# Order of the first loads in a state-space and gated-FFN kernel: activations and first weight groups dealt anew to two DMA queues

## The chip, the cores and the metric

The kernel runs on one core of a Trainium2 chip. A core has TensorE (PE, matrix products, with its weight loads PEld), VectorE (DVE), ScalarE (ACT), GpSimd (POOL), and SyncE (SP), which only issues DMA transfers here. ACT and POOL issue transfers too; each of the three has a DMA queue of its own, and the transfers of all are carried out by the core's 16 DMA engines. The metric is the device time of one execution in microseconds, as the median of several runs. The profile is of one execution, taken by the hardware profiler.

## The reference

The input x has 2048 rows of 512 elements in bfloat16. It is normalised row by row, and the sum of x and two branches is returned:

```python
xn = _layernorm(x, axis=-1)
return x + _A_ref(xn, ...) + _B_ref(xn, w_gate, w_up, w_down)

# A: a diagonal state-space layer, P = 512 complex states
Bu = jnp.einsum("bld,pd->blp", x + 0j, B_bar)
h = Lam_bar[None, :] * h + Bu[:, t, :]        # for each of the 2048 rows
y = 2.0 * jnp.einsum("blp,dp->bld", hseq, Cmat).real + x * Dskip[None, None, :]

# B: a gated feed-forward layer, F = 1376
g = _silu(x @ w_gate)
u = x @ w_up
return (g * u) @ w_down
```

## The kernel before

The 2048 rows are 16 tiles of 128 rows (`xall[:, n, :]`, tile n), and four chunks of four tiles. A chunk goes through these stages: layer norm on VectorE (`ln_stats`, `ln_rstd`, `norm_dve`, lines 174 to 189), transposition to `xnT`, the gate and up products by groups of 128 columns (`gu_mm`, line 408), the projections of the state-space layer (`bproj_tile`, line 333), rotations and scans on VectorE, and the output products (lines 488 and 497). The order on each engine is written out by hand: instructions stand on an engine in the order in which the program calls them, and a semaphore makes one wait for its inputs.

Gate and up weights are loaded in groups of columns: `fgroups = [(0, 2), (2, 4), (4, 7), (7, FT - 1)]`. Group 0 holds the column tiles 0 and 1, group 1 the tiles 2 and 3. A group of gate weights is called wg0, wg1 and so on here, a group of up weights wu0, wu1. Tiles x0 to x3 are the first chunk; a tile has 128 KB, each of the groups 0 and 1 has 256 KB, in rows of 512 bytes; rows of x have 1024 bytes. `load_w1(q, tiles, view, gi)` issues the load of group gi on the queue q; its instruction has line 112 for all groups.

The first loads are issued by SP and ACT, one behind the other on each. x0 is split over the two by partitions. Then SP issues x1, wg0, x2, wg1, x4 to x7 in one transfer, and the later groups; ACT issues wu0, x3 and wu1, and is then free for its own work. From SP's fifth load on, each issue on SP waits until the load that was issued eight loads earlier, over both queues, has landed.

The head of the program, written out at its end, is made so that TensorE can begin with single tiles of 128 rows before the chunk is complete. Eleven matmuls of 512 columns on a zeroed tile (`dummy(11, CW)`) come first. Then, in this order:

```python
    ln_stats(0)
    ln_rstd(0, 1)
    ln_stats(1)
    norm_dve(0)
    ln_rstd(1, 2)
    xT_pe(0)
    dummy(11, 128)
    ln_stats(2)
    norm_dve(1)
    ln_rstd(2, 3)
    head_mm(0, 0)
    xT_pe(1)
    head_mm(1, 0)
    head_mm(2, 0)
    ln_stats(3)
```

`ln_stats(n)` (lines 175 and 176) reads tile n and so waits for its load. `ln_rstd` is an addition on VectorE (line 179) and a power on POOL (line 180). `norm_dve(n)` (line 188) writes the normalised tile back to `xall`. On VectorE the statistics of tile n + 1 stand ahead of the normalisation of tile n. `xT_pe(n)` (line 200) transposes tile n by four matmuls into PSUM, and ACT (line 204), or VectorE for tile 3 (line 202), copies the result to `xnT`. `head_mm(fi, i)` computes column tile fi of gate and up for the 128 rows of tile i: eight matmuls of 128 columns. `head_mm(0, i)` and `head_mm(1, i)` use group 0, `head_mm(2, i)` uses group 1. The head goes on with tiles 2 and 3 in the same manner; from column tile 3 on whole chunks of 512 columns are worked on.

Of the kernel before, what the change touches and what calls it, by code (L numbers as in the profile page):

```python
# [23 lines left out]
def kernel(  # L24
# [17 lines left out]
    nc = tc.nc  # L42
# [36 lines left out]
    x_v = A_x[0].rearrange("(n p) d -> p n d", p=128)  # L79
    out_v = out[0].rearrange("(n p) d -> p n d", p=128)  # L80
    wg_v = B_w_gate.rearrange("(k p) f -> p k f", p=128)
# [3 lines left out]
    xall = const.tile([128, NT, D], BF16, name="xall")  # L85
# [3 lines left out]
    wg_g, wu_g = [], []  # L89
# [20 lines left out]
    def load_w1(q, tiles, view, gi):  # L110
        a, b = fgroups[gi]
        q.dma_start(out=tiles[gi][:], in_=view[:, :, a * 128:min(F, b * 128)])  # L112
# [1 line left out]

    nc.sync.dma_start(out=xall[0:64, 0, :], in_=x_v[0:64, 0, :])  # L115
    nc.scalar.dma_start(out=xall[64:128, 0, :], in_=x_v[64:128, 0, :])
    nc.sync.dma_start(out=xall[:, 1, :], in_=x_v[:, 1, :])  # L117
    load_w1(nc.scalar, wu_g, wu_v, 0)
    load_w1(nc.sync, wg_g, wg_v, 0)
    nc.scalar.dma_start(out=xall[:, 3, :], in_=x_v[:, 3, :])  # L120
    nc.sync.dma_start(out=xall[:, 2, :], in_=x_v[:, 2, :])
    load_w1(nc.scalar, wu_g, wu_v, 1)
    load_w1(nc.sync, wg_g, wg_v, 1)
    prm_rows = const.tile([3 * NQ, 128], BF16, name="prm_rows")
# [620 lines left out]
```

## Time and profile before

| | |
|---|---|
| median of 3 runs | 183.5 us (182.9 to 183.63) |
| profiled execution | 183.73 us, its span 181.7 us |
| PE busy | 175.3 us (96%) |
| DVE busy | 152.9 us (84%) |
| ACT busy | 93.4 us (51%) |
| POOL busy | 25.6 us (14%) |
| chain that ended last | PE 93%, DMA 3%, SPq 1%, DVE 1% |
| of it the load of x | 3.0% |
| DMA | 15.53 MB, 85 GB/s on average |

Times in the profile are microseconds from the start of the span. The chain that ended last is followed back from the last instruction, at each step to what released it. A group's idle time is that of its engine just before it, with the cause. "SPq" and "ACTq" are the issuing queues of SP and ACT; for a DMA issue, the time to landing runs from the start of the issue to the moment when the data are there. The matmuls' busy time is modelled, and pipelined matmuls overlap.

### The profile page before, as it was taken

The numbers are of one execution on the slowest core, as the hardware profiler recorded it, in microseconds if no ns is written. First come the engines' busy times: TensorE is split into PE (matmuls) and PEld (weight loads), VectorE is DVE, ScalarE is ACT, GpSimd is POOL, SyncE is SP. The second block draws the span as 40 slices with busy tenths as digits, with TensorE's granted clock in tenths as the row PEclk, the third lists the DMA queues.
The fourth block names the chain that finished last, engine by engine and source line by source line (L and its number), as shares of the span: only waits on it lengthen the run. The fifth ranks groups of instructions, "written<-read, shape, count | busy, mean of one in ns | idle before, by whom it ended". The sixth has DMA issues, their size and how long they took to land.

```text
span 181.7 us, 2449 instructions
## 1 busy us (share of the span) xinstructions
PE 175.3 (96%) x914; PEld 83.6 (46%) x914; DVE 152.9 (84%) x232; ACT 93.4 (51%) x165; POOL 25.6 (14%) x33
## 2 busy tenths in 40 slices
PE   7699999999999999999999999999999999999992
PEld 2396444444444444444444444444444444444651
DVE  2469999799999999999999999999999999940042
ACT  2158876997489869022898662014866610220000
POOL 5230200000500000026300000013405000150000
PEclk9999999999999999999999999999999999999999
DMA  4999657994034800002840000006287800062011
GB/s 118 323 277 213 132 96 179 353 180 110 0 67 99 325 4 0 0 0 32 115 87 2 0 0 4 0 0 66 36 129 98 136 0 0 3 84 33 0 58 60
DMA packets 29388, 15.53 MB, mean 85 GB/s; under 512 B 18080, under 2 KB 29312, under 8 KB 29344
## 3 DMA queue, kind: packets, MB, share of 16 engines
q1 hardware_dynamic: 24496, 11.31, 26.5%
q0 software_dynamic: 3456, 3.28, 13.6%
q10 hardware_dynamic: 1424, 0.79, 1.7%
q8 instruction: 7, 0.11, 0.3%
q14 instruction: 5, 0.04, 0.1%
HBM read 8.03 MB, written 5.24 MB: 73 GB/s over the span
## 4 chain that ended last, share of the span: by engine, by line
PE 93%; DMA 3%; SPq 1%; DVE 1%; issue 0%
PE ps L408 38%; PE ps L488 21%; PE ps L497 15%; PE ps L333 15%; DMA xall<-in_A_x_dram 3%; PE ps L434 2%; PE ps L444 1%; PE ps L200 0%; SPq L117 0%; DVE stats L175 0%; SPq L115 0%; SPq L112 0%; DVE res L500 0%; DVE xall L188 0%; DVE mv L176 0%
## 5 line engine op out<-in xcount | busy, mean ns | idle before, releaser
L408 PE MATMUL ps<-xnT,wg 128*128 128x512 bf16 (+1 forms) x196 | 42.6, 340 | 0.1
L408 PE MATMUL ps<-xnT,wu 128*128 128x512 bf16 (+1 forms) x196 | 42.6, 340 | 0.0
L488 PE MATMUL ps<-wd_sb,guT 128*128 128x512 bf16 (+3 forms) x187 | 38.7, 366 | 0.0
L375 DVE TENSOR_TENSOR_SCAN g<-r_t,car,u 128x512 bf16<-128x512 f32 x24 | 28.9, 1263 | 0.0
L497 PE MATMUL ps<-CF,wt 128*128 128x512 bf16 (+1 forms) x136 | 28.3, 366 | 0.0
L333 PE MATMUL ps<-xnT,BT 128*128 128x512 bf16 x128 | 28.3, 379 | 0.0
L488 PEld LDWEIGHTS <-guT 128*128 128x128 bf16 (+1 forms) x187 | 18.2, 98 | 20.0
L503 ACT CAST res<-ps 128x512 bf16<-128x512 f32 x12 | 7.0, 585 | 38.6 <-PE ps L497 38.6
L422 ACT ACTIVATE guT<-ps 128x512 bf16<-128x512 f32 x40 | 24.7, 618 | 4.1 <-PE ps L408 4.0
L423 ACT CAST u<-ps 128x512 bf16<-128x512 f32 x40 | 24.1, 603 | 4.3 <-PE ps L408 4.0
L408 PEld LDWEIGHTS <-wu 128*128 128x128 bf16 x196 | 17.7, 98 | 17.4
L408 PEld LDWEIGHTS <-wg 128*128 128x128 bf16 x196 | 17.5, 98 | 17.8 <-issue 1.0
L504 POOL DMA_DIRECT2D out_dram<-res x12 | 11.1, 998 | 88.0 <-ACT res L503 88.0
L497 PEld LDWEIGHTS <-wt 128*128 128x128 bf16 x136 | 13.3, 98 | 14.4
L333 PEld LDWEIGHTS <-BT 128*128 128x128 bf16 x128 | 12.5, 98 | 15.1
L335 ACT CAST u<-ps 128x512 bf16<-128x512 f32 x32 | 17.6, 588 | 3.1 <-PE ps L333 3.1
L500 DVE TENSOR_TENSOR res<-ps,xn_end 128x512 bf16<-128x512 f32 (+1 forms) x5 | 2.9, 585 | 14.9 <-PE ps L497 14.9
L175 DVE BATCH_NORM_STATS2 stats<-xall 128x6 f32<-128x512 bf16 x16 | 10.8, 673 | 4.6 <-DMA xall<-in_A_x_dram 4.6
L427 DVE TENSOR_TENSOR guT<-guT,u 128x1024 bf16<-128x1024 bf16 x20 | 13.5, 681 | 0.0
L180 POOL TENSOR_TENSOR rstd<-ve,neg_half 128x1 f32<-128x1 f32 (+1 forms) x7 | 7.6, 1082 | 41.1 <-DVE ve L179 41.1
L343 DVE TENSOR_TENSOR pm<-u,c 128x2048 bf16<-128x2048 bf16 x8 | 9.8, 1222 | 1.2 <-ACT c L260 1.1
L343 DVE TENSOR_TENSOR pm<-g,c 128x2048 bf16<-128x2048 bf16 x8 | 9.7, 1218 | 0.1
(93 smaller groups left out, 142.4 us busy)
## 6 DMA issues: line engine op xcount, KB each, us to landing
out_dram<-in_A_x_dram SPq DMA_DIRECT2D x1, 1536.0 KB, 8.3
out_dram<-res POOLq DMA_DIRECT2D x12, 128.0 KB, 3.1
out_dram<-xall POOLq DMA_DIRECT2D x3, 512.0 KB, 6.1
wd_sb<-in_B_w_down_dram SPq DMA_DIRECT2D x1, 1280.0 KB, 10.0
xall<-in_A_x_dram SPq DMA_DIRECT2D x1, 1024.0 KB, 6.1
wg<-in_B_w_gate_dram SPq DMA_DIRECT2D x2, 384.0 KB, 5.2
wu<-in_B_w_up_dram SPq DMA_DIRECT2D x2, 384.0 KB, 5.8
wu<-in_B_w_up_dram ACTq DMA_DIRECT2D x2, 256.0 KB, 5.1
```

The costliest lines, as they stand in the source:

```text
L175: nc.vector.bn_stats(out=stats[:, n, :], in_=xall[:, n, :])
L333: nc.tensor.matmul(ps[:], lhsT=BT[:, part, k, q * 128:(q + 1) * 128], rhs=xnT[:, k, c * CW:(c + 1) * CW], start=(k == 0), stop=(k == KD - 1))
L335: nc.scalar.copy(out=u_tiles[c][:, part, q, :], in_=ps[:])
L343: V.tensor_tensor(out=t[:], in0=flat(src()[:, i]), in1=flat(tab[:]), op=ALU.mult)
L375: V.tensor_tensor_scan(out=g()[:, part, q, :], data0=r_t[:, q:q + 1].to_broadcast([128, CW]), data1=u_tiles[c][:, part, q, :], initial=ini ...
L408: nc.tensor.matmul(ps[:fs, lo:hi], lhsT=wslice(groups, fi, k), rhs=xnT[:, k, c * CW + lo:c * CW + hi], start=(k == 0), stop=(k == KD - 1))
L422: nc.scalar.activation(out=guT[:fs, fi, :], in_=psg[:fs], func=ACT.Silu)
L423: nc.scalar.copy(out=u_pair[c][:fs, fi % 2, :], in_=psu[:fs])
L427: products.append(lambda: V.tensor_tensor(out=g, in0=g, in1=u, op=ALU.mult))
L488: nc.tensor.matmul(o[:], lhsT=gu_tiles[c][:fsz[fi], fi, i * 128:(i + 1) * 128], rhs=wd_sb[:fsz[fi], fi, lo:hi], start=(fi == 0), stop=False)
L497: nc.tensor.matmul(o[:], lhsT=w_tiles[c][:, part, q, i * 128:(i + 1) * 128], rhs=CF[:, part, q, lo:hi], start=False, stop=(part == 1 and q ...
L504: nc.gpsimd.dma_start(out=out_v[:, n, lo:hi], in_=res[:, lo:hi], accum_op=ALU.add)
```

## The change

The same nine loads at the head are issued in another order and in part on the other queue. SP issues its half of x0, then wg0, x2, x3, wg1; ACT issues its half of x0, then x1, wu0, wu1. x1 goes from SP to ACT, x3 from ACT to SP; wg0 moves ahead of x2 and x1; all that follows wg1 on SP stays as it is.

```diff
     nc.sync.dma_start(out=xall[0:64, 0, :], in_=x_v[0:64, 0, :])
     nc.scalar.dma_start(out=xall[64:128, 0, :], in_=x_v[64:128, 0, :])
-    nc.sync.dma_start(out=xall[:, 1, :], in_=x_v[:, 1, :])
+    load_w1(nc.sync, wg_g, wg_v, 0)
+    nc.scalar.dma_start(out=xall[:, 1, :], in_=x_v[:, 1, :])
+    nc.sync.dma_start(out=xall[:, 2, :], in_=x_v[:, 2, :])
     load_w1(nc.scalar, wu_g, wu_v, 0)
-    load_w1(nc.sync, wg_g, wg_v, 0)
-    nc.scalar.dma_start(out=xall[:, 3, :], in_=x_v[:, 3, :])
-    nc.sync.dma_start(out=xall[:, 2, :], in_=x_v[:, 2, :])
+    nc.sync.dma_start(out=xall[:, 3, :], in_=x_v[:, 3, :])
     load_w1(nc.scalar, wu_g, wu_v, 1)
     load_w1(nc.sync, wg_g, wg_v, 1)
```

## The prediction

> **What bounds the kernel now.** I read the chain that ended last first, then the timeline of the first 14 us by engine, then the DMA issues window by window with their time to landing, then the byte rate of those 14 us. The chain (start, length, what) says that one load and then TensorE alone set the end:
>
> ```profile
> 2.72 5.37 DMA xall<-in_A_x_dram
> ...
> 8.11 0.71 DVE stats L175
> ...
> 9.40 0.38 PE ps L200 x4
> 9.78 1.34 PE ps L408 x24
> ...
> 178.25 0.02 issue
> 178.27 0.42 DVE res L500
> ```
>
> From 9.4 us to 178.25 us the chain holds PE pieces only. So any time by which the work at 9.4 us starts sooner comes off the end, if nothing behind it runs dry; and nothing but this head can be moved by a change of the first loads. The 5.37 us load is x2, issued at 2.72 us by SP. VectorE (start, length, what, idle time before it and its cause) shows which loads it waits for:
>
> ```profile
> 3.25 0.70 DVE L175 BATCH_NORM_STATS2 stats<-xall 128x6 f32<-128x512 bf16 x1 [2.10 <-DMA xall<-in_A_x_dram]
> 4.20 0.15 DVE L179 TENSOR_SCALAR ve<-mv 128x1 f32<-128x1 f32 x1
> 5.58 0.69 DVE L175 BATCH_NORM_STATS2 stats<-xall 128x6 f32<-128x512 bf16 x1 [1.23 <-DMA xall<-in_A_x_dram]
> 8.11 0.69 DVE L175 BATCH_NORM_STATS2 stats<-xall 128x6 f32<-128x512 bf16 x1 [1.26 <-DMA xall<-in_A_x_dram]
> 9.30 0.68 DVE L175 BATCH_NORM_STATS2 stats<-xall 128x6 f32<-128x512 bf16 x1
> 10.31 0.41 DVE L188 TENSOR_SCALAR xall<-xall,mv,rstd 128x512 bf16<-128x512 bf16 x1
> ```
>
> Tiles x0, x1 and x2 are each waited for; x3 (9.30) is not. The timeline of TensorE has the other half: a hole before the transposes of x1's tile, and none after it.
>
> ```profile
> 9.38 0.40 PE L200 MATMUL ps<-ident,xall 128*128 128x128 bf16 x4 [0.86 <-DVE ve L179]
> 10.01 0.27 PEld L408 LDWEIGHTS <-wg 128*128 128x128 bf16 x4
> 10.90 0.27 PEld L200 LDWEIGHTS <-xall 128*128 128x128 bf16 x4
> ```
>
> The 10.01 us row is the first use of gate group 1 (head_mm(2, 0)); 10.90 us is the transposes of tile 2.
>
> **In which order loads land.** Issue time plus time to landing, from the windows of the DMA issues (queue, KB, us to landing; here the window from 2.6 to 3 us for the first three, the one from 3 to 3.5 us for the last):
>
> ```profile
> wg<-in_B_w_gate_dram SPq DMA_DIRECT2D x1, 256.0 KB, 4.7
> wu<-in_B_w_up_dram ACTq DMA_DIRECT2D x1, 256.0 KB, 5.8
> xall<-in_A_x_dram SPq DMA_DIRECT2D x1, 128.0 KB, 5.4
> ```
> ```profile
> wg<-in_B_w_gate_dram SPq DMA_DIRECT2D x1, 256.0 KB, 5.9
> ```
>
> That is wg0 2.25 + 4.7 = 6.95, wu1 2.52 + 5.8 = 8.3, x2 8.09, wg1 3.27 + 5.9 = 9.17. The neighbouring windows give x0 3.1, x1 1.39 + 4.2 = 5.6, wu0 1.34 + 4.4 = 5.7, x3 1.96 + 4.1 = 6.06, x4 to x7 3.74 + 6.9 = 10.6. In the packet records the two queues take turns, one whole load each: x0, wu0 (ACT), x1 (SP), x3 (ACT), wg0 (SP), wu1 (ACT), x2 (SP), then SP's rest. So what counts is how many KB are ahead on both queues together: 512 KB including itself land at 5.6, 640 at 6.06, 896 at 6.95, 1152 and 1280 at 8.1 to 8.3, 1536 at 9.17.
>
> **The change, part by part.** It adds and removes no instruction. The order of instructions of both programs differs in three places on SP and two on ACT, and on no other engine. By the same turns the new order is x0 (128 KB so far), x1 256, wg0 512, wu0 768, x2 896, wu1 1152, x3 1280, wg1 1536.
>
> x1, formerly 512 KB deep, is 256 deep. Between 128 KB at 3.1 and 512 KB at 5.6 that is about 3.9 us. VectorE is free at 4.35 (4.20 + 0.15). Its statistics start then; the normalisation of tile 0 comes 0.83 later, as before (6.41 - 5.58), at 5.18, ends at 5.56. TensorE is in its eleven warming matmuls until 5.99, so the transposes of tile 0 go from 6.85 to 5.99. ACT's copy and the first head_mm follow 0.86 us sooner, at 7.06; wu0 (between 6.06 and 6.95, so 6.5) and wg0 (5.6) are there. If SP were served first, x1 would keep its 5.6 us, and VectorE would be free for tile 2 at 6.86 instead: no cost, since x2 ends later.
>
> x2, formerly 1280 KB deep, is 896 deep: 6.95 instead of 8.09, a gain of 1.14. From its statistics to tile 1's transposes are 9.38 - 8.11 = 1.27, so these start at 8.24.
>
> x3 goes from 640 to 1280 KB deep: 8.1 instead of 6.06. Its cover was 9.30 - 6.06 = 3.2 us; now VectorE asks for it at 6.97 + 1.19 = 8.16. It is just in time. This is the edit costed at nothing: without cover, each us that x3 is late moves VectorE's tile 2, because tile 3's statistics stand ahead of tile 2's normalisation on that engine. Normalisation of tile 2 ends at 8.16 + (10.72 - 9.30) = 9.58.
>
> wg1 keeps its 1536 KB: 9.17. Before, it had a cover of 10.01 - 9.17 = 0.84. TensorE would now reach it at 8.24 + 0.63 = 8.87, so it waits, and this new wait ends last: 9.20 instead of 10.01 is 0.81 gained. Tile 2's transposes come 0.89 later, 10.09, after their 9.58.
>
> What of SP's later issues: the next weight groups and the B transposes each wait for a load eight issues back. These land within 0.2 us of what they did (wg0 at 5.6 where x1 was; x2 at 6.95 where wg0 was; x3 at 8.1 where x2 was), and x4 to x7 land at 10.6 for a use at 14.47, three us of cover after the shift. Nothing.
>
> One term is unknown: how fast the first half MB flows. Byte rate in 40 slices of 0.35 us:
>
> ```profile
> GB/s 0 0 0 0 0 15 193 186 80 97 260 328 379 358 338 345 336 299 287 315 312 299 309 319 347 347 337 339 337 320 329 323 323 292 223 56 167 250 290 275
> ```
>
> Between 2.8 and 3.5 us only some 88 GB/s flow, against 330 later; in these slices wu0 with its 512 B rows was alone. Lost there: 0.7 x (1 - 88/330) = 0.51 us. With x1's 1024 B rows in that place nothing, or all of this, may be won: 0 to 0.51; if wg0's rows then bring one more such slice, it is 0.26 worse. I take the rate in rows to stay and the rows to be twice as long, which moves 62 KB more, or 0.19 us. The sum: 0.81 + 0.19 = **1.0 us**, ends 0.55 and 1.32. The profiled execution of 183.73 us with its span of 181.7 becomes 182.7 with 180.7; the median of the runs shown is 0.23 lower, so 182.5.
>
> The Trainium skill, page "DMA: Bandwidth & Descriptors", section "Rules for kernel authors", speaks against such edits: spreading loads over issuing engines does not help, since all run on the same 16 DMA engines. By it alone the time would stay at 183.5; the rows above agree that wg1's landing does not move, but show that the turns decide which load comes first. The same page's "Specifications" give some 358 GB/s per core from HBM; wg1's 1.57 MB would by that take 4.4 us from 2.1 on and bind nothing; tile 1's transposes would stand right behind head_mm(0, 0), and an estimate by the page gives a gain of 1.9, 181.6. The 300 GB/s or so of the slices after 5.9 us are against it.
>
> **The rivals.** (a) Eaten by late weights: wg1 lands at 9.5 to 10.0 instead of 9.17. Each tenth costs a tenth: at 9.8 the gain is 0.2, 183.3. For it: the wait is new and decides everything. Against: its place in the sequence is the same. (b) The start of the DMA stream is cured: 1.32 gained, 182.2. For it: the 88 GB/s are a loss at wu0 alone. Against: x0's own rate was 190 GB/s, with 1024 B rows, not 330. (c) Slower: x3 is not served in turn but with x4 to x7, which follow it on SP. Tile 3's statistics then block VectorE, and tile 2's transposes come 1.42 + 0.06 after x3. Up to a landing at 9.42 this is no slower than before (10.90); at 10.6 it costs 1.2, 184.7. For it: x3 is the load with the most cover before and the least after. Against: 768 KB lie between 8.1 and that landing. That the change does not take place is excluded by the order of instructions.
>
> **How the numbers follow.** Forecast 0.61, with its own range of 182.2 to 182.9; (a) 0.20, (b) 0.12, (c) 0.07. A measurement of this kernel can tell 0.5%, or 0.92 us, from no change (the three runs lie 0.73 apart), so the line stands at 182.58. The forecast lies on it: about two thirds of it, 0.40, and (b) give faster 0.52; the rest of it, (a) and a little of (c) give same 0.42; slower is 0.06. The range is 182.0 to 183.2: it takes in (b) and most of (a), and leaves out (c) and single tails.
>
> **What would show it.** x1 lands by 4.5 and x2 near 6.9; VectorE's wait for x2 is below 1.3 us and over by 7.0; TensorE's transposes of tile 0 stand directly behind the warming matmuls at 6.0, those of tile 1 near 8.2; then a hole of 0.3 us that ends with wg1's landing near 9.0 to 9.2; after it an unbroken TensorE chain, 1.0 us shorter in its end. It is wrong if x2 lands after 7.5, if x3 lands after 8.5, or if TensorE waits again behind the head, as for BT at about 21 us.

## The result, and the profile after

| | before | changed |
|---|---|---|
| median of 20 runs | 183.52 us (182.62 to 184.46) | 182.73 us (182.32 to 183.26) |
| profiled execution | 183.73 us, span 181.7 | 182.59 us, span 180.6 |

The ratio is 0.9963, with a 95% interval of 0.995 to 0.9977. The change makes the kernel faster by 0.79 us in the medians, 1.0 us had been forecast. The 20 runs of the kernel before are not of one kind: seven of them, 182.62 to 183.08, lie within the range of the changed kernel, and as no such run was profiled, what made them shorter is open. The two profiled spans differ by 1.1 us. The chain that ended last in the changed kernel (start, length, what):

```profile
1.36 4.09 DMA xall<-in_A_x_dram
...
5.48 0.70 DVE stats L175
...
7.18 0.59 ACT xnT L204
...
7.82 0.61 PE ps L408 x8
8.42 0.22 PE ps L200 x4
8.65 1.34 PE ps L408 x24
...
177.14 0.42 DVE res L500
```

The last output comes 1.13 us sooner (178.27 before), and all of this is made in the head: TensorE's unbroken stretch now starts at 7.82 us. The load in the chain is another one, too: x1, issued by ACT at 1.36 us, and no longer x2. VectorE (start, length, what, idle before and its cause) shows it:

```profile
5.48 0.69 DVE L175 BATCH_NORM_STATS2 stats<-xall 128x6 f32<-128x512 bf16 x1 [1.12 <-DMA xall<-in_A_x_dram]
6.67 0.68 DVE L175 BATCH_NORM_STATS2 stats<-xall 128x6 f32<-128x512 bf16 x1
7.85 0.68 DVE L175 BATCH_NORM_STATS2 stats<-xall 128x6 f32<-128x512 bf16 x1
```

The wait for x1 is still there (before, it ended at 5.58); the one for x2, which ended at 8.11, is gone; and x3, at 7.85, isn't waited for. On TensorE:

```profile
6.75 0.40 PE L200 MATMUL ps<-ident,xall 128*128 128x128 bf16 x4 [0.68 <-DVE ve L179]
8.26 0.39 PE L200 MATMUL ps<-ident,xall 128*128 128x128 bf16 x4
8.88 0.27 PEld L408 LDWEIGHTS <-wg 128*128 128x128 bf16 x4
```

Tile 1's transposes come at 8.26 instead of 9.38, and the first use of gate group 1 at 8.88 instead of 10.01. No hole stands before that use, though wg1 had landed only just before. It was issued at 3.26, and its row in the window of DMA issues from 3.5 to 4 us gives 5.6 us to landing, so 8.86:

```profile
xall<-in_A_x_dram SPq DMA_DIRECT2D x1, 512.0 KB, 6.8
wg<-in_B_w_gate_dram SPq DMA_DIRECT2D x1, 256.0 KB, 5.6
```

That is 0.3 us sooner than the 9.17 before, with the same KB ahead of it (both are sums with a row of one decimal). The byte rate in slices of 0.35 us is to be held against the row shown of before:

```profile
GB/s 0 0 0 0 0 3 199 186 106 124 179 255 368 362 343 329 348 274 331 325 294 307 279 320 334 351 353 338 342 327 336 325 320 308 253 113 228 289 255 4
```

The two slow slices (2.8 to 3.5 us) now move 106 and 124 GB/s, and not 80 and 97; but the climb behind them is slower, 179 and 255 instead of 260 and 328. Summed to 8.4 us, 1726 KB have moved, and 1769 before. The stream is no faster, then. In the packet records, half of the packets of wg1 have ended at 7.47 us, and before at 7.36; but the last one ends at 8.28 instead of 8.51. Its last packets trail less behind the others.

### The profile page after: what moved, and what is told of

The parts are those of the page before. It is cut to its first block, busy times and chain, and to the rows that moved or that the text cites. A ratio compares the mean times of both kernels' runs of the same rounds, so it can differ in the third digit from the quotient of the medians.

```text
span 180.6 us, 2449 instructions
## 1 busy us (share of the span) xinstructions
PE 175.2 (97%) x914; PEld 83.5 (46%) x914; DVE 152.8 (85%) x232; ACT 93.4 (52%) x165; POOL 25.5 (14%) x33
## 4 chain that ended last, share of the span: by engine, by line
PE 94%; DMA 2%; DVE 1%; ACT 0%; ACTq 0%; issue 0%
PE ps L408 39%; PE ps L488 21%; PE ps L497 15%; PE ps L333 15%; DMA xall<-in_A_x_dram 2%; PE ps L434 2%; PE ps L444 1%; PE ps L200 1%; DVE stats L175 0%; ACT xnT L204 0%; ACTq L116 0%; DVE res L500 0%; DVE xall L188 0%; DVE mv L176 0%; PE ps L225 0%
```

## The experiments

Two kernels keep everything but the loads. For the others a second family was made, in which the 28 DMA transposes (of B, C, and of the normalised tiles of chunks 1 to 3) are plain copies of the same sizes; what these bring is not transposed there. A family's kernels are compared with each other. "Outside" is the time of a run less its span. Unless said otherwise, diffs are against the changed kernel.

### x1 given back to SP

```diff
-    load_w1(nc.sync, wg_g, wg_v, 0)
-    nc.scalar.dma_start(out=xall[:, 1, :], in_=x_v[:, 1, :])
-    nc.sync.dma_start(out=xall[:, 2, :], in_=x_v[:, 2, :])
+    nc.sync.dma_start(out=xall[:, 1, :], in_=x_v[:, 1, :])
     load_w1(nc.scalar, wu_g, wu_v, 0)
+    load_w1(nc.sync, wg_g, wg_v, 0)
+    nc.sync.dma_start(out=xall[:, 2, :], in_=x_v[:, 2, :])
```

> The changed kernel with x1 given back to SP, ahead of wg0. By turns: x1 256 KB deep, wu0 512, wg0 768, wu1 1024, x2 1152, x3 1280, wg1 1536 (SP's half of x0 first), or wu0 384, x1 512, wu1 768, wg0 1024, x2 1152 (ACT's first). x2 is deep again and lands at 7.8 to 8.1: VectorE waits for it over 1 us as before, TensorE's transposes of tile 1 stand at 9.1 to 9.4, and the time is that of before less at most 0.3: 183.2 to 183.5. Rival, that the depth of x2 does not matter and the sooner issue of x1 does: 182.7 or less.

183.4 us (12 runs), ratio to before 0.9998 (0.9984 to 1.0011): the gain is gone. VectorE and TensorE of this kernel:

```profile
5.13 0.69 DVE L175 BATCH_NORM_STATS2 stats<-xall 128x6 f32<-128x512 bf16 x1 [0.75 <-DMA xall<-in_A_x_dram]
7.77 0.69 DVE L175 BATCH_NORM_STATS2 stats<-xall 128x6 f32<-128x512 bf16 x1 [1.36 <-DMA xall<-in_A_x_dram]
```
```profile
9.04 0.40 PE L200 MATMUL ps<-ident,xall 128*128 128x128 bf16 x4 [0.92 <-DVE ve L179]
```

x1 is even sooner here than in the changed kernel's trace (5.13, not 5.48), and it buys nothing, as x2 is deep again and comes at 7.77. So x2's place decides, as forecast.

### The first three tiles ahead of all weights

```diff
-    nc.sync.dma_start(out=xall[0:64, 0, :], in_=x_v[0:64, 0, :])
-    nc.scalar.dma_start(out=xall[64:128, 0, :], in_=x_v[64:128, 0, :])
-    load_w1(nc.sync, wg_g, wg_v, 0)
-    nc.scalar.dma_start(out=xall[:, 1, :], in_=x_v[:, 1, :])
-    nc.sync.dma_start(out=xall[:, 2, :], in_=x_v[:, 2, :])
+    nc.scalar.dma_start(out=xall[:, 0, :], in_=x_v[:, 0, :])
+    nc.sync.dma_start(out=xall[:, 1, :], in_=x_v[:, 1, :])
+    nc.scalar.dma_start(out=xall[:, 2, :], in_=x_v[:, 2, :])
+    load_w1(nc.sync, wg_g, wg_v, 0)
```

> x0 in one piece on ACT, x1 first on SP, x2 second on ACT, then wg0 (SP), wu0 (ACT), x3 (SP), wu1 (ACT), wg1 (SP): the first three tiles are the first 384 KB, so x1 lands near 3.5 and x2 near 5. TensorE's transposes of tile 0 then stand right behind the warming matmuls at 6.0 to 6.1, head_mm(0, 0) at 7.15 instead of 7.82, tile 1's transposes near 7.6 instead of 8.2. If wg1 binds (my theory) TensorE waits there: a hole of about 0.6 us before head_mm(2, 0) that ends with wg1's landing near 8.9, and no gain over the changed kernel, 182.7 within 0.2. Rival, that x1's landing bounds the changed kernel alone: 0.6 faster, 182.1.

181.79 us (6 runs), ratio to before 0.9911 (0.9892 to 0.9929). The time is a miss: 0.94 below the changed kernel where nothing was expected. The account of the head held, though: tile 1's transposes came at 7.63, and TensorE then stood still twice, 0.25 us each, before a first use of group 1 at 8.55 and 9.03:

```profile
8.55 0.23 PEld L407 LDWEIGHTS <-wg 128*128 128x128 bf16 x4 [0.26 <-DMA wg<-in_B_w_gate_dram]
9.02 0.23 PEld L407 LDWEIGHTS <-wu 128*128 128x128 bf16 x4 [0.24 <-DMA wu<-in_B_w_up_dram]
```

Its last output, begun at 177.02, is only 0.12 sooner than in the changed kernel's trace. The rest lies elsewhere: 0.4 us less from the end of that output to the end of the span (2.62 for 3.00), and 1.77 us outside for 2.03. This is the fastest kernel here with the transposes in it. It joins two edits, as x0 is in one piece too; that one is taken alone below.

### The family's base, and the change in it

> The kernel before with its 28 DMA transposes (of B, C and of the normalised tiles of chunks 1 to 3) replaced by plain copies of the same sizes, so that what they bring is not transposed. It is the base of a family of kernels with plain copies. All of them are off the chain that ended last, so the head's times and the whole should stay: 183.5, within 0.4, and VectorE's wait for x2 ends near 8.1 us. If a transpose was on the path after all, faster by more than 0.5.

> The changed kernel, with plain copies in place of the 28 DMA transposes, as in the kernel of the last sentence's family: the data that these bring are not transposed. 182.7, within 0.4, and 0.8 below the family's kernel before, if the gain is made in the head alone. If the transposes (which the change makes SP issue a little sooner or later) have part in the gain, the two of the family differ by less than 0.4.

183.59 us and 182.52 us (10 runs each), spans 181.55 and 180.5 in the median: 1.07 us between them. So the gain doesn't hang on the transposes. The changed kernel's trace here differs from the other in one thing. There, SP's half of x0 sent its first packets at 2.10 us and ACT's at 2.37; here ACT's came at 2.09, and SP's at 2.35. VectorE and TensorE's weight loads of this kernel:

```profile
4.28 0.68 DVE L175 BATCH_NORM_STATS2 stats<-xall 128x6 f32<-128x512 bf16 x1
5.10 0.38 DVE L188 TENSOR_SCALAR xall<-xall,mv,rstd 128x512 bf16<-128x512 bf16 x1
6.49 0.69 DVE L175 BATCH_NORM_STATS2 stats<-xall 128x6 f32<-128x512 bf16 x1 [0.95 <-DMA xall<-in_A_x_dram]
7.89 0.69 DVE L175 BATCH_NORM_STATS2 stats<-xall 128x6 f32<-128x512 bf16 x1
```
```profile
8.65 0.23 PEld L408 LDWEIGHTS <-wg 128*128 128x128 bf16 x4 [0.23 <-DMA wg<-in_B_w_gate_dram]
```

x1 isn't waited for at all (issued at 1.34, landed 2.6 later, at 3.9), x2 is waited for until 6.49, and the new wait is there: 0.23 us for wg1, which lands at 8.6. For x3, too, VectorE stands still a little: it was issued at 2.79 and landed 5.1 later, at 7.9, and the engine, free since 7.76 (7.61 + 0.15), begins at 7.89. The view names idle time only from 0.15 us on, so the row shows no wait. The two queues had moved 289 KB by 3.5 us where the family's kernel before had moved 212, but by 5 us 701 for 688: the gain at the start is given back at once. The same kernel once more, as the base of the last experiment, gave 182.76 us (6 runs), 0.24 above the first set and a little outside what was expected. In its trace ACT's half is again first, x1 landed at 3.9, and the first use of wg1 comes at 8.71:

> The changed kernel of the family of plain copies (in place of the 28 DMA transposes) once more, as the base of the next run on the same chip: 182.5 within 0.2, span 180.5. If ACT's half of x0 is first in its trace, x1 lands near 3.9 and a hole before head_mm(2, 0) ends with wg1 near 8.6; if SP's half is first, x1 lands near 5.5, x2 near 5.8, and there is no such hole.

### x3 behind wg1

```diff
-    nc.sync.dma_start(out=xall[:, 3, :], in_=x_v[:, 3, :])
     load_w1(nc.scalar, wu_g, wu_v, 1)
     load_w1(nc.sync, wg_g, wg_v, 1)
+    nc.sync.dma_start(out=xall[:, 3, :], in_=x_v[:, 3, :])
```

> As the changed kernel of this family (plain copies in place of the DMA transposes), with x3 issued behind wg1 on SP: 1536 KB deep, landing near 8.9 us. It prices the cover that x3 lost. VectorE asks for x3 at 7.85, then waits some 1.0 us; normalisation of tile 2 ends 1.42 after x3, near 10.3, and TensorE's transposes of tile 2 start near 10.35 instead of 9.77: 0.55 slower than the family's changed kernel, 183.3. Rival, that weights bind and x3 has cover: no change or faster by up to 0.2, since wg1 lands 0.4 sooner.

182.94 us (10 runs), 0.42 above the family's changed kernel. VectorE, then TensorE:

```profile
8.80 0.69 DVE L175 BATCH_NORM_STATS2 stats<-xall 128x6 f32<-128x512 bf16 x1 [0.95 <-DMA xall<-in_A_x_dram]
```
```profile
10.28 0.40 PE L200 MATMUL ps<-ident,xall 128*128 128x128 bf16 x4 [0.69 <-DVE xall L188]
```

VectorE waits 0.95 us for x3, and TensorE waits for VectorE: the cover of x3 is used up in the changed kernel, to within what was forecast.

### x3 given back to ACT

```diff
-    nc.sync.dma_start(out=xall[:, 3, :], in_=x_v[:, 3, :])
+    nc.scalar.dma_start(out=xall[:, 3, :], in_=x_v[:, 3, :])
```

> The changed kernel in the family of plain copies, with x3 given back to ACT between wu0 and wu1: the moves of x1 and wg0 alone. x2 keeps 640 to 896 KB, so the gain should stay: VectorE's statistics of tile 2 begin near 6.5 to 6.7, tile 1's transposes at 7.8 to 8.2; wu1 is now last with 1536 KB, near 8.6 to 8.9 for a use at 8.9 to 9.1. 182.5 within 0.2, span 180.5. Rival, that x3's move off ACT makes the gain (by sooner up weights): span 181.0 or more.

182.84 us (10 runs), span 180.8 in the median: between the two theories. That is 0.3 slower than the base of 182.52, but only 0.08 above the base's second set of 182.76. In its trace:

```profile
7.26 0.69 DVE L175 BATCH_NORM_STATS2 stats<-xall 128x6 f32<-128x512 bf16 x1 [1.44 <-DMA xall<-in_A_x_dram]
```
```profile
10.17 0.40 PE L408 MATMUL ps<-xnT,wu 128*128 128x128 bf16 x4 [0.58 <-DMA wu<-in_B_w_up_dram]
```

wu1 is now the last load of ACT's queue and lands at 10.1 (3.11 + 7.0), not at 8.9. SP's queue has one load less ahead of x4 to x7, whose 512 KB are under way at the same time. The last output begins at 178.17, as late as in the family's kernel before (178.14); only a shorter time behind it, 2.50 us instead of 3.00, keeps this execution below that one. So in this execution the moves of x1 and wg0 alone bring nothing to the last output, while in the medians most of the gain stays (182.84 against 183.59 of the family's kernel before). x3's move to SP may have a part of its own, by keeping x4 to x7 behind group 1. This isn't shown: the profiled run is one of the longer ones (183.12), and the trace also has loads late that stand ahead of x3, wg0 at 6.8 (base: 5.7) and x2 at 7.2 (base: 6.5).

### x0 in one piece

```diff
-    nc.sync.dma_start(out=xall[0:64, 0, :], in_=x_v[0:64, 0, :])
-    nc.scalar.dma_start(out=xall[64:128, 0, :], in_=x_v[64:128, 0, :])
+    nc.sync.dma_start(out=xall[:, 0, :], in_=x_v[:, 0, :])
```

> As the changed kernel of this family (plain copies in place of the DMA transposes), with x0 in one piece on SP, so that x1 is the first load of ACT and next in turn: x1 lands near 3.5 us and not 5.5; x2, x3 and wg1 keep their depths of 640 to 896, 1280 and 1536 KB. TensorE's transposes of tile 0 follow the warming matmuls at 6.1 (6.75 in the changed kernel). If x1 bounded the changed kernel in its trace, the work gets 0.4 to 0.65 faster, until wu1 or wg1 binds near 8.9. If wg1's landing bounds it, as I had predicted, not more than 0.15 faster. Beside that, the kernel with x0 in one piece that ran before had 0.27 us less outside its span and 0.4 us less behind its last output; if one load less is the cause, both are seen here too.

181.81 us (10 runs), 0.71 below its base: 0.26 of it outside the span (1.78 for 2.04), some 0.5 in it. In the trace the last output is 0.38 sooner. Neither account given fits as it stands. x1 had landed at 3.9 in the base as well, and TensorE doesn't wait for wg1: issued at 2.68, it lands 5.6 later, near 8.28, and TensorE, busy until then, uses it at 8.28. The chain that ended last goes through x2, VectorE, and tile 1's transposes:

```profile
6.32 0.69 DVE L174 BATCH_NORM_STATS2 stats<-xall 128x6 f32<-128x512 bf16 x1 [0.81 <-DMA xall<-in_A_x_dram]
7.59 0.40 PE L199 MATMUL ps<-ident,xall 128*128 128x128 bf16 x4 [0.40 <-DVE ve L178]
```

So x2 bounds the head in this trace, with wg1 just in time behind it. What moved is the whole stream: 1824 KB by 8 us, and 1633 in the base. A half of x0 takes 0.56 to 0.60 us to issue here, the whole tile 0.39 to 0.41, and the first packets come at 1.78 instead of 2.09.

To see whether the 0.26 us come from one transfer less, the load of x4 to x7 was cut in two:

```diff
-    nc.sync.dma_start(out=xall[:, TPC:2 * TPC, :], in_=x_v[:, TPC:2 * TPC, :])
+    nc.sync.dma_start(out=xall[:, TPC:TPC + 2, :], in_=x_v[:, TPC:TPC + 2, :])
+    nc.sync.dma_start(out=xall[:, TPC + 2:2 * TPC, :], in_=x_v[:, TPC + 2:2 * TPC, :])
```

> As the kernel with x0 in one piece, and the load of x4 to x7 cut in two halves of two tiles each, so that the number of transfers is again that of the changed kernel. If the smaller time outside the span (1.78 instead of 2.04) and behind the last output comes from one transfer less, both go back: 2.04 outside, time 0.26 to 0.6 longer than with x0 in one piece. If they come from x0 being in one piece, nothing changes: 181.8.

The time outside went back to 2.0 us, so that part follows the number of transfers. The time didn't rise, against the expectation: 181.85 us, but over only 4 runs that spread from 181.69 to 182.52. The longest of them was profiled, and has the clearest row of the new wait:

```profile
8.81 0.40 PE L408 MATMUL ps<-xnT,wg 128*128 128x128 bf16 x4 [0.36 <-DMA wg<-in_B_w_gate_dram]
```

### TensorE's use of group 1 put off

Two kernels with the first three tiles ahead of the weights, without and with this edit of TensorE's order:

```diff
     head_mm(1, 0)
-    head_mm(2, 0)
...
-    head_mm(0, 1)
     xT_pe(2)
+    head_mm(0, 1)
...
     head_mm(1, 1)
+    head_mm(2, 0)
     head_mm(2, 1)
```

> The kernel with x0 on ACT, x1 on SP, x2 on ACT and then the weights, once more, with plain copies in place of the 28 DMA transposes: the base for the next one. As with transposes, 181.8 within 0.3, span 180.05; TensorE waits twice behind tile 1's transposes (7.6 us), for wg1 near 8.5 and for wu1 near 9.0, some 0.5 us together. If my account of this is wrong, no such holes.

> The same loads and plain copies, with TensorE's order changed in the head: head_mm(2, 0), the first user of wg1 and wu1, moves from behind tile 1's products to behind head_mm(1, 1), and tile 2's transposes move ahead of head_mm(0, 1). No load is changed. If the landing of group 1 bounds the kernel with early x, the two holes (0.5 us) go, less up to 0.2 that tile 2's normalisation (ends at 8.32) may cost: 181.4, 0.3 to 0.5 below its base. Rival, that the head is bounded by x or by VectorE: no change, within 0.15.

182.05 us (182.01 to 182.21) and 181.58 us (181.3 to 181.76), 4 runs each: 0.47 faster. (The first is no faster than the kernel with x0 in one piece alone, 181.81: the early tiles add nothing to that.) The waits of TensorE in the first of them:

```profile
7.59 0.40 PE L407 MATMUL ps<-xnT,wu 128*128 128x128 bf16 x4 [0.31 <-DMA wu<-in_B_w_up_dram]
9.38 0.40 PE L407 MATMUL ps<-xnT,wu 128*128 128x128 bf16 x4 [0.50 <-DMA wu<-in_B_w_up_dram]
```

In the second, neither stands: head_mm(2, 0) comes at 9.61, behind work that was ready. So with early tiles the landing of the weights is the bound. Part of the difference between the two traces isn't the edit's: wu0 landed at 6.6 in the second trace and at 7.6 in the first, with the same loads.

The same edit on the changed kernel's own loads:

> The changed kernel's loads (plain copies in place of the DMA transposes), with TensorE's order in the head changed as in the deferring kernel before: head_mm(2, 0) behind head_mm(1, 1), tile 2's transposes ahead of head_mm(0, 1). It prices the new wait for wg1 in the changed kernel itself. By the hole of its trace it is worth 0.2 us where ACT's half is first and nothing else: 0.1 to 0.2 faster than its base, 182.35. If wg1 held back the changed kernel by what the prediction says (wg1 0.3 us later than TensorE could use it), 0.3; if it is no bound, 0 or, since tile 2's normalisation ends near 9.3, up to 0.2 slower.

183.44 us (12 runs) against 182.76 of its base: 0.7 slower, a miss. The edit took the wait for wg1 away and put a greater one in its place:

```profile
9.59 0.40 PE L200 MATMUL ps<-ident,xall 128*128 128x128 bf16 x4 [0.68 <-DVE xall L188]
```

Tile 2's normalisation isn't ready there before 9.5 us, and head_mm(0, 1), which was, now stands behind it. The edit changes two places in the order; this run doesn't price the wait for wg1 alone.

## Why the prediction was right, and where it was off

**The head alone, carried to the end.** Right, between the two traces: 1.12 us at tile 1's transposes, 1.13 at the first use of wg1, 1.13 at the last output.

**The turns of whole loads.** Right in the traces where ACT's half of x0 goes first, as in the trace of before: x1 at 3.9 (forecast 3.9), x2 at 6.5 to 6.8 (6.95); the kernel with x3 on ACT is outside of this, with x2 at 7.2. In the changed kernel's own trace SP's half went first: wg0 landed at 5.2, x1 at 5.5, x2 at 5.8. Which queue is first is not set by the program's order, and I had taken it from one trace. So three of the signs named in the prediction are missing there, x1 by 4.5 us, tile 0's transposes at 6.0 and the hole that ends with wg1; the family's two traces of the change have them, at 3.9, at 5.9 and 6.0, and with 0.2 us.

**"If SP were served first ... no cost."** This sentence failed. VectorE was free of it, as argued, but TensorE wasn't: tile 0's transposes stayed at 6.75 and the first head_mm came at 7.82, not at 7.06. Tile 1's transposes, whose data were ready at 7.87, had to queue behind it until 8.26. It stayed hidden in the sum, as x2 landed sooner in this order than forecast (5.8, not 6.95): TensorE reached wg1's first use at 8.88, against 8.87 in the sum. That two errors cancel to 0.01 us is luck.

**x2 decides.** Right: with x2 deep again, in the kernel with x1 given back to SP, the time is that of before. Once x2 is early, though, it bounds only some of the traces; the changed kernel's own is bound by x1. Tile 1's transposes were forecast at 8.24, and stand at 8.26 in one order (for another reason) and at 7.76 in the other.

**x3 just in time.** Right: in the family's trace it lands at 7.9 for statistics at 7.89, after some 0.1 us of waiting that costs TensorE nothing (tile 2's normalisation ends at 9.31, its transposes come at 9.56); in the changed kernel's own it lands at 7.1 for 7.85. With x3 one place later the kernel lost 0.42 us. The rival in which x3 is served with x4 to x7 did not occur. What I hadn't priced is that x3's place on SP holds those four tiles back; whether that is worth anything stays open.

**wg1 as the new wait.** Right as a mechanism: waits of 0.23 and 0.36 us stand in the traces of the family, and of 0.5 us for wu1 where the tiles come early. In the changed kernel's own trace there was no such wait: wg1 landed near 8.86, and TensorE came to it at 8.88, by way of x1.

**The start of the stream.** The term of 0.19 us (bounds -0.26 and 0.51) came out near 0.3, as wg1 landed at 8.86 instead of 9.17. That 0.81 and 0.3 add up to the 1.1 us of the trace is in part luck, as wg1 wasn't what TensorE waited for. And the step behind the term failed. In the changed kernel's own trace x1 wasn't in the slow slices at all, as SP's wg0 was first. In the family's trace it was, and moved 77 KB more by 3.5 us, where 62 were forecast; but by 5 us 13 of them were left. wg1 came sooner because its last packets trailed less; why is open.

**The size.** The medians, 0.79, give less than the 1.1 of the traces. Of the difference, 0.3 is the place of the two profiled executions in their spreads: the span of before was 181.7, and 17 later spans of that kernel have a median of 181.5; the 20 spans of the changed kernel have one of 180.7, its profiled one 180.6. The forecast of 1.0 was made on one execution at the long side of its kind, which may be why it lay above; this isn't shown, and the family's pair gave 1.07 in its medians. The measured 182.73 also falls short of the line at 182.58, on the side that the prediction gave 0.42 and not 0.52.

The rule that spreading loads over issuing engines doesn't help (Trainium skill, "DMA: Bandwidth & Descriptors", "Rules for kernel authors") speaks of bandwidth, and there the sums of bytes agree (1726 KB by 8.4 us, 1769 before). As a forecast of the time, 183.5, it failed: the order of landing was worth 0.79 us. The estimate of 181.6 by the page's 358 GB/s failed too: wg1 landed at 8.6 to 8.9, and not at 6.5. The same "Rules for kernel authors" say of two transfers to disjoint halves of the partitions, don't bother. The run with x0 in one piece agrees: 0.71 us faster, 0.26 of it outside the span.

## What to carry to other kernels

In this kernel the loads at the head are one sequence over both queues. For such a head, write down how many KB are ahead of each, when it lands and when it is first used, and give the first places to what is used first; then look for the next load that comes just in time, since it bounds what the edit can bring. Where two queues start level, cost both orders of their turns through every engine. And try a first tile in one piece: cut in two over the queues, it cost 0.71 us here.

## What was not expected of the hardware

Which of two queues that issue at the same time sends first differs between executions of the same head: ACT's at 2.08 to 2.09 us and SP's at 2.35 to 2.37 in eight traces with x0 in halves, the reverse (2.10 and 2.37) in one. That this makes the spread of the runs was not shown.

As the first load of its queue, a half tile of 64 partitions took longer to issue (0.56 to 0.61 us) than a whole one of 128 with twice the bytes (0.39 to 0.41).

The time outside the span was 1.73 to 1.83 us in the kernels with one transfer less, and 1.98 to 2.11 in the others. The time from the end of the last output to the end of the span was 2.5 to 2.6 us in four kernels, and 3.0 to 3.1 in all others, whatever the number of transfers; its cause is open.
